# A two-stage kernel whose split operands move to rows 0 and 64 and whose instruction order comes from a planner of its own

## The chip, the cores and the metric

The kernel runs on one core of one Trainium2 chip. The metric is the device time of one execution in microseconds (us); the time before is the median of three runs. A core has five instruction queues that each run in order: TensorE (PE, with its weight loads shown as PEld), VectorE (DVE), ScalarE (ACT), GpSimd (POOL) and SyncE (SP, which here issues all DMAs).

## The reference

Inputs r, k, v, w, a, b have the shape 4 batches x 8 heads x 768 steps x 40. A 40x40 state per batch and head is carried through 768 steps, and its readings go through two dense blocks.

```python
for t in range(S):
    y[:, :, t] = np.einsum('bhd,bhde->bhe', rt, state)
    Sa = np.einsum('bhde,bhe->bhd', state, at)
    state_decay = state * wt[:, :, None, :] - np.einsum('bhd,bhe->bhde', Sa, bt)
    state = state_decay + np.einsum('bhd,bhe->bhde', vt, kt)
...
h = x @ w_in;  g = h * (1.0 / (1.0 + np.exp(-h)));  x = g @ w_out     # first block, 320 -> 2048 -> 320
h = x @ w_in;  g = h - np.tanh(h);                  return g @ w_out  # second block, own weights
```

The weights of the blocks arrive as 64-bit floats; the output is 3072 x 320 in fp32.

## The kernel before

The 768 steps are cut into 12 chunks of 64. Within a chunk the recurrence is solved with matrix products, so that only the 40x40 states pass from chunk to chunk. The 32 states (batch x head) are two halves `hf` of 16, and a half is two groups `u` of 8. Most fp32 factors are split into a high and a low fp16 number.

The stages of a chunk are small functions inside `build`, which are also the names used below. `load_raw` and `prep` bring in the inputs, form running products of w (two scans on DVE), scale the factors and split them into the tile HL; 24 DMAs per chunk then lay HL out as the tile LR. `p1` and `p2` multiply and transpose these factors on PE. `sol_in`, 31 times `sol_step` (two DVE instructions each, one waiting for the other) and `sol_out` solve a triangular system; `mrg1` and `mrg2` merge its 32-row blocks. Then comes the chain that carries the state: `ch_x` (PE) and `ch_xe` (ACT), `ch_u` (PE) and `ch_ue` (ACT and DVE, writes U), `ch_s` and `ch_se`, `ch_y` and `ch_ye` (writes the next transposed state MT), `ch_m` and `ch_me` (writes the next state M). `x_t1` and `x_t2` transpose the readings into the first block: `mm_h` (16 matmuls per hidden slice i of 8), `act1` (three ACT passes and one on POOL), `mm_o` (12 matmuls per i), `out1`, whose result goes to DRAM. When all chunks are done the second block runs: `mm_h`, `act2` and `mm_o` again, for 12 groups of tokens.

L (columns 0 to 193 of LR: decayed k and b, and u or v) and R (columns 194 to 321: a and r) hold three planes on 120 rows. L has high, high, low and R has high, low, high on rows 0 to 39, 40 to 79 and 80 to 119, so that one matmul with 120 rows sums high x high, high x low and low x high. MT and M have the same three planes. `ch_ue`, `ch_ye` and `ch_me` write the high plane to rows 0 to 39 and the low plane to a tile `lows`, and two DMAs each copy them to rows 40 to 79 and 80 to 119:

```python
ACT.activation(out=U[0:40, u], in_=pu, func=AF.Copy, scale=S_U)                                   # L398
DVE.scalar_tensor_tensor(out=Ul[:, u], in0=pu, scalar=S_U, in1=U[0:40, u], op0=ALU.mult, ...)     # L399
for p0, src in ((40, U[0:40]), (80, Ul)):
    SP.dma_start(out=U[p0:p0 + 40]..., in_=src...)                                                # L401
```

Two things set the order of instructions. The functions are called in the order of a time that the table `SC` gives each (8 units to a chunk, L687 onward); the framework's own scheduler, which has a model of the engines, then orders the instructions of each queue. The conversion of the first block's weights (`conv_w1`, 32 calls of `conv_f32` and what follows it) is tied behind instructions of chunk 0 (`gates`). LR tiles come from a ring of 5 buffers, which the second block's weights (`conv_w2`) use after chunk 11.

Of the kernel before, what the change touches and what calls it, by code (L numbers as in the profile page):

```python
# [9 lines left out]
I32 = mybir.dt.int32  # L10
# [14 lines left out]
RW = LW + 2 * C  # L25

# [80 lines left out]
def build(tc, pk, tv, w1i, w1o, w2i, w2o, out, nch=NCH, dbg=None):  # L107
# [16 lines left out]
    lrp = top.enter_context(tc.tile_pool(name="lrp", bufs=5))  # L124
# [14 lines left out]
    istk = const.tile([120, 40], F16, name="istk")  # L139
    POOL.memset(istk, 0.0)  # L140
    for base in (0, -80):
        POOL.affine_select(out=istk, in_=istk, compare_op=ALU.not_equal, fill=1.0, base=base,
                           pattern=[[-1, 40]], channel_multiplier=1)
# [20 lines left out]
    TT_t = [at_p.tile([128, 32, C], F32, name=f"TT{q}") for q in range(2)]  # L164
    mK_t = [at_p.tile([128, 4, 8, C], F32, name=f"mK{q}") for q in range(2)]
    for q in range(2):
        POOL.memset(mK_t[q][64 * q:64 * q + 64], 0.0)
        DVE.memset(TT_t[q], 0.0)
    VU_s = [at_p.tile([128, 2, DM], F32, name=f"VU{q}") for q in range(2)]
    Xs_s = [at_p.tile([128, 8, D], F32, name=f"Xs{q}") for q in range(4)]  # L170
# [4 lines left out]
    zo = const.tile([128, 2], F32, name="zo")  # L175
    POOL.memset(zo[:, 0:1], 0.0)
    POOL.memset(zo[:, 1:2], 1.0)
    tmp = at_p.tile([128, 136], F32, name="tmp")

    lows = at_p.tile([104, 32 * D], F16, name="lows")  # L180
    HL = at_p.tile([120, 6, 2 * RW], F16, name="HL")

    def planes(HL):
        return [HL[:, :, o:o + n] for o, n in ((0, LW), (LW, 2 * C), (RW, LW), (RW + LW, 2 * C))]

    DVE.memset(planes(HL)[0][:, :, 3 * C:LW], 0.0)
# [4 lines left out]
    gates = {}  # L191
# [9 lines left out]
    def load_raw(c, hf):  # L201

        spare = lr_slot().rearrange("p u n -> p (u n)").bitcast(F32)[0:120] if c == 0 and hf == 1 else None
# [12 lines left out]
    def prep(c, hf):  # L216
        w, ra, rkb, rrv = raw_t.pop((c, hf))
        hl = HL
        if c == 0 and hf == 1:
            hl = lr_slot().rearrange("p u n -> p (u n)")[0:120, 0:12 * RW].rearrange("p (j n) -> p j n", j=6)  # L220
            DVE.memset(planes(hl)[0][:, :, 3 * C:LW], 0.0)
# [48 lines left out]
    def p1(c, b):  # L270
# [47 lines left out]
    def sol_step(c, j):  # L318
# [5 lines left out]
        if c == 0:  # L324
            gates["dve"] = nc.cur_bb.bb.instructions[-1]

    def sol_out(c):
# [3 lines left out]
        TT = TT_t[c % 2]  # L331
# [28 lines left out]
    def mrg2e(c, hf):  # L360
        bb = 64 * (c % 2)
        ACT.activation(out=TT_t[c % 2][bb:bb + 32, hf * 16:hf * 16 + 16, 32:64], in_=ps_t["mg2", c][64 * hf:64 * hf + 32],
                       func=AF.Copy)

    def ch_x(c, hf):
        ps = ps_a.tile([128, 8, D], F32, tag="a", name="psx")
        for p in range(8):
            if c:
                for u in range(2):
                    PE.matmul(ps[64 * u:64 * u + 64, p, :], R_t[c, hf][:, u, p, 0:C], MT_t[c, hf][:, u, p, :], start=True, stop=False)  # L370
# [5 lines left out]
    def ch_xe(c, hf):  # L376
        bb = 64 * (c % 2)
        ps = ps_t.pop(("x", c, hf))
        for u in range(2):
            t = Xs_s[(4 * c + 2 * hf + u) % 4]  # L380
# [3 lines left out]
    def ch_u(c, hf):  # L384
        t = [ps_t.pop(("Xs", c, hf, u)) for u in range(2)]
        ps = ps_a.tile([128, 8, C], F32, tag="a", name="psu")
        for p in range(8):
            for u in range(2):
                PE.matmul(ps[64 * u:64 * u + 40, p, :], t[u][:, p, :], TT_t[c % 2][:, hf * 16 + u * 8 + p, :], start=True, stop=True)
        ps_t["u", c, hf] = ps  # L390

    def ch_ue(c, hf):
        ps = ps_t.pop(("u", c, hf))
        U_t[c, hf] = lows[0:40, 0:16 * C].rearrange("p (u j n) -> p u j n", u=2, n=C)
        U, Ul = L_t[c, hf][:, :, :, C:2 * C], U_t[c, hf]
        for u in range(2):
            pu = ps[64 * u:64 * u + 40]
# [397 lines left out]
```

## Time and profile before

| | |
|---|---|
| median of 3 runs | 1195.06 us (1190.68 to 1195.49) |
| the profiled execution | 1191.78 us, of which the span is 1190.0 us |
| mean granted TensorE clock | 0.924 of 2.4 GHz |
| PE / DVE / ACT / POOL busy | 78% / 72% / 74% / 43% of the span |
| PE weight loads busy | 63% of the span |

The span has four parts. Up to 173 us there is almost no dense work: chunk 0 is computed and the weights are converted. From there to 785 us the other chunks and the first block run side by side. Then follows the rest of the first block with the first matmuls of the second, to 874 us, and the second block alone to the end. The busy time of matmuls is modelled at its end, so that a PE that is always busy can still be waiting a little before each short matmul.

### The profile page before, as it was taken

The page shows a single profiled execution, that of the slowest core. Times are in us where ns is not written, and L with a number is a line of the kernel's source. Part 1 is how long each engine was busy: PE and PEld are TensorE (multiplying, and loading weights), DVE is VectorE, ACT ScalarE, POOL GpSimd, SP SyncE. Part 2 cuts the span into 40 slices and gives each one's busy share as a digit, 9 for nine tenths or more (in the row PEclk, how much of TensorE's full clock was granted, in tenths as well). Part 3 has the DMA queues.
Part 4 walks back from the last instruction along what each step waited for, and adds up shares of the span by engine and source line. Part 5 has one row for each costly group of instructions (what it writes and reads, how often), then busy time and mean ns, then how long its engine had stood idle before and what let it go on. Part 6 is the DMA issues. An engine that isn't in the chain of part 4 may idle for free.

```text
span 1190.0 us, 32101 instructions
## 1 busy us (share of the span) xinstructions
PE 930.4 (78%) x12624; PEld 754.0 (63%) x12624; DVE 860.6 (72%) x1752; ACT 886.4 (74%) x1718; POOL 508.7 (43%) x550
## 2 busy tenths in 40 slices
PE   0004327878888888897888888888999999999997
PEld 0004326657766666676766766776778888888885
DVE  6677878677877687787778757443188878888885
ACT  2468689757676677576757798998678888888885
POOL 5354564444444454454544334444333333333332
PEclk9999559888889898999889999999989999999999
DMA  6676765444435444445444333344011111111001
GB/s 161 183 199 176 187 171 140 111 118 117 125 99 138 107 119 115 123 113 124 115 108 123 79 105 96 108 124 120 14 27 37 25 26 25 26 31 32 13 12 23
DMA packets 181192, 115.85 MB, mean 97 GB/s; under 512 B 107121, under 2 KB 165553, under 8 KB 181041
## 3 DMA queue, kind: packets, MB, share of 16 engines
q1 hardware_dynamic: 181040, 113.80, 36.5%
q8 instruction: 99, 1.62, 0.6%
q14 instruction: 53, 0.43, 0.1%
HBM read 58.34 MB, written 12.58 MB: 60 GB/s over the span
## 4 chain that ended last, share of the span: by engine, by line
issue 20%; DMA 17%; PE 16%; ACT 15%; DVE 14%; SPq 10%; POOL 9%; POOLq 0%; DVEq 0%; ACTq 0%
POOL gl L196 7%; SPq L256 6%; PE hp L576 6%; DMA LR<-HL 4%; DMA pd<-pq 3%; ACT cr L532 2%; DVE tmp L321 2%; PE o L602 2%; DVE Tl L323 2%; PE o L600 2%; DMA LR<-lows 2%; PE o L601 2%; DVE pq L230 2%; DVE lows L399 2%; DMA x2d<-x2o 1%
## 5 line engine op out<-in xcount | busy, mean ns | idle before, releaser
L576 PE MATMUL hp<-xh,wih 128*128 128x256 f16 x960 | 196.4, 292 | 19.5 <-ACT hs L585 19.5
L196 POOL TENSOR_TENSOR gl<-q,gh 128x512 f16<-128x512 f32 x96 | 111.9, 1167 | 205.6 <-ACT gh L635 205.6
L576 PE MATMUL hp<-x,LR 128*128 128x256 f16 x1344 | 188.7, 274 | 1.9 <-DVE t L633 1.2
L196 POOL TENSOR_TENSOR gl<-hs,gh 128x512 f16<-128x512 f32 x96 | 113.9, 1186 | 150.0 <-ACT hs L587 100.0
L576 PEld LDWEIGHTS <-wih 128*128 128x128 f16 x1344 | 134.1, 104 | 46.2 <-issue 21.2
L576 PEld LDWEIGHTS <-LR 128*128 128x128 f16 x1344 | 132.1, 98 | 25.0 <-issue 2.4
L602 PE MATMUL o<-woh,gl 128*128 128x320 f16 x384 | 113.2, 308 | 8.6 <-POOL gl L196 8.5
L600 PE MATMUL o<-woh,gh 128*128 128x320 f16 x384 | 117.2, 307 | 3.3 <-ACT gh L586 2.1
L601 PE MATMUL o<-woh,gh 128*128 128x320 f16 x384 | 116.6, 306 | 0.0
L600 PE MATMUL o<-LR,gh 128*128 128x320 f16 x384 | 112.9, 302 | 1.3 <-ACT gh L635 1.3
L601 PE MATMUL o<-LR,gh 128*128 128x320 f16 x384 | 113.9, 302 | 0.0
L576 PE MATMUL hp<-xl,wih 128*128 128x256 f16 x384 | 112.2, 292 | 0.0
L321 DVE TENSOR_TENSOR tmp<-Al,Tl 128x126 f32<-128x126 f32 (+22 forms) x372 | 92.5, 249 | 19.2 <-ACT Al L312 10.0
L602 PE MATMUL o<-LR,gl 128*128 128x320 f16 x384 | 104.3, 302 | 0.5 <-POOL gl L196 0.5
L323 DVE TENSOR_TENSOR Tl<-Tl,tmp 128x126 f32<-128x126 f32 (+22 forms) x372 | 95.9, 258 | 9.1
L602 PEld LDWEIGHTS <-gl 128*128 128x128 f16 x768 | 75.4, 99 | 37.5 <-POOL gl L196 12.5
L630 DVE SCALAR_TENSOR_TENSOR s<-s,z 128x512 f32<-128x512 f32 x96 | 74.4, 775 | 33.2 <-ACT s L628 32.2
L600 PEld LDWEIGHTS <-gh 128*128 128x128 f16 x768 | 76.5, 100 | 31.9 <-ACT gh L586 2.7
L632 DVE SCALAR_TENSOR_TENSOR q<-hp,s 128x512 f32<-128x512 f32 x96 | 66.3, 691 | 38.2 <-POOL gl L196 26.2
L601 PEld LDWEIGHTS <-gh 128*128 128x128 f16 x768 | 76.3, 99 | 27.8 <-issue 1.4
L634 DVE COPY_PREDICATED q<-mk,t 128x512 f32<-128x512 int32 x96 | 79.2, 825 | 9.0
L276 PE MATMUL p1a<-LR 120*128 120x64 f16 x384 | 23.3, 211 | 78.6 <-DMA LR<-HL 54.6
(148 smaller groups left out, 2563.3 us busy)
## 6 DMA issues: line engine op xcount, KB each, us to landing
LR<-HL SPq DMA_DIRECT2D x92, 150.9 KB
rawkb<-pk SPq DMA_DIRECT2D x23, 360.0 KB
rawrv<-pk SPq DMA_DIRECT2D x23, 360.0 KB
cr<-w1i SPq DMA_DIRECT2D x16, 384.0 KB
cr<-w2i SPq DMA_DIRECT2D x16, 384.0 KB
cr<-w1o SPq DMA_DIRECT2D x16, 320.0 KB
cr<-w2o SPq DMA_DIRECT2D x16, 320.0 KB
LR<-HL SPq DMA_DIRECT2D x46, 100.6 KB
```

Source lines behind the costliest of these rows:

```text
L196: POOL.tensor_tensor(out, a, b, ALU.subtract)
L230: DVE.tensor_tensor_scan(pt[:, 0:390], w[:, 0:390], d1a.rearrange("p j t -> p (j t)"), 0.0, ALU.mult, ALU.add)
L256: SP.dma_start(out=dst[pl * 40:pl * 40 + 40, :, d0:d0 + w], in_=src[:, :, s0:s0 + w])
L321: DVE.tensor_tensor(tv_, Al[:, j + 1:, j:j + 1].to_broadcast([128, n, w]), Tl[:, j:j + 1, :w].to_broadcast([128, n, w]), ALU.mult)
L323: DVE.tensor_tensor(Tl[:, j + 1:, :w], Tl[:, j + 1:, :w], tv_, ALU.add)
L576: PE.matmul(o, wi[f][:, a], x[:, k], start=n == 0, stop=False)
L600: PE.matmul(o, gh[:, cs], wo[f][:, 0], start=f == 0, stop=False)
L601: PE.matmul(o, gh[:, cs], wo[f][:, 1], start=False, stop=False)
L602: PE.matmul(o, gl[:, cs], wo[f][:, 0], start=False, stop=f == NF - 1)
L630: DVE.scalar_tensor_tensor(out=s, in0=s, scalar=GAMMA, in1=z, op0=ALU.add, op1=ALU.mult)
L632: DVE.scalar_tensor_tensor(out=q, in0=hp, scalar=sh * S_G2, in1=s, op0=ALU.mult, op1=ALU.mult)
L634: DVE.copy_predicated(q, mk.bitcast(I32), t)
```

## The change

Four things change. The planes move: high on rows 0 to 39, low on rows 64 to 103, and rows 40 to 63 are zeroed once, so a product has 104 rows. R becomes two operands, R[0] with the high plane in both places and R[1] with the low plane in both, and each product with R takes two matmuls (`for q in range(2)`), which now sum all four combinations. ACT, DVE and POOL write U, MT and M straight into both places, and the 136 copies by DMA are gone; a layout of HL in 18 instead of 24 DMAs per chunk follows. In `ch_ue` and `ch_me` a call `apart` declares ACT's reading of group 1 independent of DVE's reading of group 0 in the same PSUM bank. LR is 4 fixed buffers (`LRS`) instead of a ring of 5, so chunk c's `prep` follows `ch_y` of chunk c - 2, and the second block's weights lie 5 to a buffer: numbers 0 to 4 in LRS[0], and so on, number 15 in LRS[3], which chunk 11's second half uses. MT and M have one buffer per half, Xs eight instead of four, TT one.

The order is planned. `kernel` builds the program three times: once to get its instructions and their dependencies, from which `plan` gives an order of the calls; once in that order, from which `plan` gives a sequence for each of the five queues, DMA issues included; and once more with each instruction of the first part of the program tied to its predecessor in its sequence. `plan` takes, again and again, the instruction with the longest way to the end among those that could start soonest, on the engine that is free first, with written costs per instruction. The second block (after `ph1.close()`) is not planned. `gates` is gone; `BOOST` puts `conv_w1` first.

```diff
+RX = RW + 2 * C
...
-    TT_t = [at_p.tile([128, 32, C], F32, name=f"TT{q}") for q in range(2)]
+    TT = at_p.tile([128, 32, C], F32, name="TT")
...
+    LRS = [lrp.tile([128, 16, RX], F16, name=f"LR{q}") for q in range(4)]
+    MTS = [at_p.tile([104, 2, 8, D], F16, name=f"MT{q}") for q in range(2)]
+    MS = [at_p.tile([104, 2, 8, D], F16, name=f"M{q}") for q in range(2)]
...
-            for pl, s0, d0, w in ((0, RW, 0, LW), (0, LW, LW, 2 * C), (1, RW, 0, RW), (2, 0, 0, RW)):
-                SP.dma_start(out=dst[pl * 40:pl * 40 + 40, :, d0:d0 + w], in_=src[:, :, s0:s0 + w])
...
+            for p0, s0, d0, w in ((0, 0, 0, RX), (64, LW, LW, 4 * C), (64, RX, 0, 3 * C)):
+                SP.dma_start(out=dst[p0:p0 + 40, :, d0:d0 + w], in_=src[:, :, s0:s0 + w])
+        LR = LR[0:104].rearrange("p (u j) n -> p u j n", u=2)
+        L, R = LR[:, :, :, 0:LW], (LR[:, :, :, LW:RW], LR[:, :, :, RW:RX])
...
-            PE.matmul(pa[:, p, :], kb, R[:, u, p, 0:C], start=True, stop=True)
+            for q in range(2):
+                PE.matmul(pa[:, p, :], kb, R[q][:, u, p, 0:C], start=q == 0, stop=q == 1)
...
+            for q in range(2 if c else 0):
                 for u in range(2):
-                    PE.matmul(ps[64 * u:64 * u + 64, p, :], R_t[c, hf][:, u, p, 0:C], MT_t[c, hf][:, u, p, :], start=True, stop=False)
+                    PE.matmul(ps[64 * u:64 * u + 64, p, :], R_t[c, hf][q][:, u, p, 0:C], MTS[hf][:, u, p, :], start=q == 0, stop=False)
...
         for u in range(2):
-            pu = ps[64 * u:64 * u + 40]
-            ACT.activation(out=U[0:40, u], in_=pu, func=AF.Copy, scale=S_U)
-            DVE.scalar_tensor_tensor(out=Ul[:, u], in0=pu, scalar=S_U, in1=U[0:40, u], op0=ALU.mult, op1=ALU.subtract)
-        for p0, src in ((40, U[0:40]), (80, Ul)):
-            SP.dma_start(out=U[p0:p0 + 40].rearrange("p u j n -> p (u j) n"), in_=src.rearrange("p u j n -> p (u j) n"))
+            pu, U = ps[64 * u:64 * u + 40], L_t[c, hf][:, u, :, C:2 * C]
+            i = ACT.activation(out=U[0:40], in_=pu, func=AF.Copy, scale=S_U)
+            if u:
+                apart(i, last)
+            last = DVE.scalar_tensor_tensor(out=U[64:104], in0=pu, scalar=S_U, in1=U[0:40], op0=ALU.mult, op1=ALU.subtract)
...
-            PE.matmul(ps[:, p, :], uv, R_t[c, hf][:, u, p, C:2 * C], start=True, stop=True)
+            for q in range(2):
+                PE.matmul(ps[:, p, :], uv, R_t[c, hf][q][:, u, p, C:2 * C], start=q == 0, stop=q == 1)
...
-                psub(ml[:, u], md, MT[0:40, u])
-            SP.dma_start(out=MT[40:80], in_=MT[0:40])
-            SP.dma_start(out=MT[80:120], in_=ml)
+                psub(MT[64:104, u], md, MT[0:40, u])
...
-        SP.dma_start(out=M[40:80], in_=M[0:40])
-        SP.dma_start(out=M[80:120], in_=ml)
...
+            last = DVE.tensor_tensor(M[64:104, u], pu, M[0:40, u], ALU.subtract)
...
-            t = lr_slot().rearrange("p u n -> p (u n)")[:, 0:4 * 1280].rearrange("p (f n) -> p f n", f=4)
-            w2.extend(t[:, q] for q in range(4))
+            t = LRS[f // 5].rearrange("p u n -> p (u n)")[:, 0:5 * 1280].rearrange("p (f n) -> p f n", f=5)
+            w2.extend(t[:, q] for q in range(5))
...
+BOOST = {"conv_w1": 100000}
+SPLIT = {"h1": 8, "o1": 6}
...
+    while any(ready.values()):
+        best = None
+        for e, r in ready.items():
...
+        t, n = max((q for q in c if q[0] <= t + LOOK[e]), key=lambda q: (us[q[1]].rank, -q[1]))
...
+        if e == "DVE" and u.two:
+            if busy[0] <= t < busy[1]:
+                f = max(f, busy[1] + min(u.cost, 90))
...
+    order, _ = traced(None)
+    _, seq = traced(order)
...
+        for _, v in seq:
+            for x, y in zip(v, v[1:]):
+                tc.add_manual_dep(ins[y], ins[x].name, info, reason="planned order")
```

Three places show what moves. On PE, where `ch_y` ends and `ch_s` of the next group begins, before (psm is the state's product, pss the product of U and v with R, psu their transpose by an identity `istk`):

```order
L431 MATMUL psy<-M,LR 64x40
L442 MATMUL psm<-VU_127,KBt 40x40 x15
L409 LDWEIGHTS LR
L409 MATMUL pss<-LR 128x64
L410 LDWEIGHTS LR
L410 MATMUL psu_4959<-istk,LR 128x40
```

and such a place now:

```order
L449 MATMUL psm<-VU_125,KBt 40x40 x16
L416 LDWEIGHTS LR_152
L416 MATMUL pss<-LR_152 128x64
L416 LDWEIGHTS LR_152
L416 MATMUL pss<-LR_152 128x64
L417 LDWEIGHTS LR_152
L417 MATMUL psu_6418<-istk,LR_152 128x40
```

The same weights are loaded twice, and the product with R is two matmuls.

On SP, in the middle of the program before, where U is copied (L401), the dense block's result leaves (L613), the next HL is laid out (L256) and MT is copied (L457, L458):

```order
L401 DMA LR<-lows 40x16x64
L613 DMA x2d<-x2o 128x2x384
L256 DMA LR<-HL 40x6x194
L256 DMA LR<-HL 40x6x128
L213 DMA VU_127<-tv 64x640
L256 DMA LR<-HL 40x6x322 x2
L256 DMA LR<-HL 40x6x194
L256 DMA LR<-HL 40x6x128
L256 DMA LR<-HL 40x6x322
L457 DMA MT<-MT 40x640
L256 DMA LR<-HL 40x6x322
L458 DMA MT<-lows 40x640
```

and such a place now (L268 lays out HL, L494 and L496 fetch factors for `x_t2`, L623 is the dense block's result):

```order
L268 DMA LR_151<-HL 40x6x192 x2
L268 DMA LR_151<-HL 40x4x192
L494 DMA pf<-pd 128x2x128
L496 DMA pf<-pd 64x128
L623 DMA x2d<-x2o 128x2x384
L268 DMA LR_151<-HL 40x6x450
L268 DMA LR_151<-HL 40x6x256
L268 DMA LR_151<-HL 40x6x450
L268 DMA LR_151<-HL 40x6x256
L268 DMA LR_151<-HL 40x4x450
L268 DMA LR_151<-HL 40x4x256
L226 DMA VU_125<-tv 64x640
```

No copy of U, MT or M stands in the queue any more; every DMA in it brings in inputs, lays out HL or carries a result away.

On DVE, at the start before, after the memsets (L230 to L245 are `prep` of chunk 0):

```order
L230 SCALAR_TENSOR_TENSOR pq<-raww,d1a 120x390
L231 RECIPROCAL d1b<-pq 120x6
L232 TENSOR_SCALAR HL<-pq 120x6
L235 SCALAR_TENSOR_TENSOR rawa<-rawa,pq 120x384
L236 SCALAR_TENSOR_TENSOR pr<-raww,d1b 120x389
L233 SCALAR_TENSOR_TENSOR HL<-pq,HL 120x6
L239 TENSOR_TENSOR rawkb<-rawkb,pr 120x768
```

and now (L535 and L537 belong to `conv_f32`, the conversion of weights):

```order
L242 SCALAR_TENSOR_TENSOR pq<-raww,d1a 120x390
L535 TENSOR_SCALAR cr<-cr 128x384
L243 RECIPROCAL d1b<-pq 120x6
L247 SCALAR_TENSOR_TENSOR rawa<-rawa,pq 120x384
L248 SCALAR_TENSOR_TENSOR pr<-raww,d1b 120x389
L537 SCALAR_TENSOR_TENSOR c_174<-c_174,cr 128x384
L251 TENSOR_TENSOR rawkb<-rawkb,pr 120x768
```

Weight conversion stands among the very first instructions, where before it began only with chunk 1's `prep`; by the end of chunk 0's part (`x_t2` of its second half) DVE has passed 19 whole pairs of it, against 27 before.

## Rows read from the trace of the kernel before

**Rows 1.** The page: busy times, 40 slices (PE, clock, GB/s), one costly group.
```profile
PE 930.4 (78%) x12624; PEld 754.0 (63%) x12624; DVE 860.6 (72%) x1752; ACT 886.4 (74%) x1718; POOL 508.7 (43%) x550
...
PE   0004327878888888897888888888999999999997
...
PEclk9999559888889898999889999999989999999999
...
GB/s 161 183 199 176 187 171 140 111 118 117 125 99 138 107 119 115 123 113 124 115 108 123 79 105 96 108 124 120 14 27 37 25 26 25 26 31 32 13 12 23
...
L276 PE MATMUL p1a<-LR 120*128 120x64 f16 x384 | 23.3, 211 | 78.6 <-DMA LR<-HL 54.6
```

**Rows 2.** Stages: length; busy us (instructions) per engine; granted clock, DMA share, GB/s.
```profile
0.00:173.00 173.00, 35.87 (x722) 32.21 (x724) 125.28 (x278) 102.56 (x197) 83.18 (x115) 0.84 0.67 177
173.00:261.00 88.00, 66.22 (x1139) 52.87 (x1133) 65.77 (x159) 68.23 (x135) 41.97 (x43) 0.87 0.52 136
261.00:478.00 217.00, 181.20 (x3081) 148.65 (x3079) 162.72 (x373) 151.34 (x304) 98.78 (x103) 0.89 0.44 115
478.00:654.00 176.00, 146.59 (x2530) 118.06 (x2528) 135.71 (x310) 120.29 (x245) 83.02 (x83) 0.92 0.46 118
654.00:785.00 131.00, 112.20 (x1922) 91.30 (x1920) 81.51 (x215) 113.65 (x234) 56.44 (x72) 0.96 0.36 100
785.00:874.00 89.00, 79.30 (x720) 63.20 (x719) 34.27 (x59) 69.52 (x134) 37.03 (x45) 0.94 0.26 72
874.00:1190.00 316.00, 309.00 (x2534) 247.71 (x2532) 255.35 (x363) 260.78 (x474) 108.26 (x93) 0.99 0.12 26
```

**Rows 3.** Timeline of DVE: the first U written in chunk 2 and chunk 9.
```profile
251.33 0.68 DVE L399 SCALAR_TENSOR_TENSOR lows<-psu,LR 40x512 f16<-40x512 f32 x1
...
666.21 0.68 DVE L399 SCALAR_TENSOR_TENSOR lows<-psu,LR 40x512 f16<-40x512 f32 x1
```

**Rows 4.** Waits: who waited for whom, us in total, times, longest.
```profile
PE p1a L276 <- DMA LR<-HL: 54.6, 8, 22.7
...
PE mg L342 <- DVE W L333: 49.1, 5, 28.3
...
ACT LR L398 <- DVE lows L399: 33.2, 14, 4.4
...
PE pss L409 <- DMA LR<-lows: 27.8, 11, 13.6
```

**Rows 5.** The critical chain in order of time: start, us, what.
```profile
495.75 2.80 DMA LR<-lows
```

**Rows 6.** Tile lows: SP's own time per DMA, ns min/median/max, first and last start.
```profile
L401 SPq DMA_DIRECT2D LR<-lows x24: 767/798/1056, 122.7 to 785.8; - x24
L458 SPq DMA_DIRECT2D MT<-lows x22: 731/757/868, 143.1 to 757.9; - x22
```

**Rows 7.** Timeline of PE: start, us until a run's last matmul ends, shape, count.
```profile
479.92 0.20 PE L370 MATMUL psx<-MT,LR 120*64 120x40 f16 x2
...
479.95 0.29 PE L372 MATMUL psx<-VU,mK 128*64 128x40 f32 x4
...
528.75 0.40 PE L276 MATMUL p1a<-LR 120*128 120x64 f16 x8
...
645.92 0.64 PE L276 MATMUL p1a<-LR 120*128 120x64 f16 x8
```

**Rows 8.** Groups of DVE instructions: count, busy us, mean ns, idle before them.
```profile
L533 DVE SCALAR_TENSOR_TENSOR c<-c,cr 128x384 int32<-128x384 int32 (+1 forms) x64 | 37.2, 582 | 25.0 <-ACT cr L532 23.4 <-POOL wih L196 0.8 <-POOL x2o L612 0.5
...
L230 DVE TENSOR_TENSOR_SCAN pq<-raww,d1a 120x390 f32<-120x390 f32 x23 | 32.8, 1425 | 5.7 <-DMA pd<-pq 4.0 <-DMA raww<-pk 1.3
...
L531 DVE TENSOR_SCALAR cr<-cr 128x384 int32<-128x384 int32 (+1 forms) x64 | 26.5, 418 | 26.8 <-ACT c L530 26.4
...
L168 DVE MEMSET TT<- 128x2048 f32 x2 | 3.5, 1765 | 1.7 <-PEq L786 1.3 <-issue 0.4
```

**Rows 9.** Line L230 by itself: ns min/median/max, first and last start.
```profile
L230 DVE TENSOR_TENSOR_SCAN pq<-raww,d1a x23: 970/1212/2362, 9.2 to 640.2; 120x390 f32<-120x390 f32 x23
```

More of the change, by code (lines that the diff above doesn't have):

```diff
@@ L167, in build @@
         POOL.memset(mK_t[q][64 * q:64 * q + 64], 0.0)
-        DVE.memset(TT_t[q], 0.0)
     VU_s = [at_p.tile([128, 2, DM], F32, name=f"VU{q}") for q in range(2)]
-    Xs_s = [at_p.tile([128, 8, D], F32, name=f"Xs{q}") for q in range(4)]
+    Xs_s = [at_p.tile([128, 8, D], F32, name=f"Xs{q}") for q in range(8)]
     for t in VU_s + Xs_s:
@@ new lines, in latency_of, with units_of @@
+def latency_of(i, e, cost):
+    if e == "PE":
+        return cost + 170
+    if e == "SP":
+        o = i.outs[0]
+        name = o.bass_ap.tensor.name
+        return 4300 if name[:3] in ("raw", "cr_", "VU_") or name.startswith("LR") and o.ap[0][1] != 40 else 3000
+    return cost
+class Unit:
+    __slots__ = ("e", "ins", "cost", "late", "succ", "pred", "rank", "ready", "name", "args", "tiles", "tiled", "two", "left", "hold", "holds", "start")
+def units_of(tc, ins, marks):
+    at = {i.name: k for k, i in enumerate(ins)}
+    n1 = marks[-1][0]
+    task = [(-1, "init", ())] * n1
+    for (a, nm, ar), (b, _, _) in zip(marks, marks[1:]):
+        task[a:b] = [(a, nm, ar)] * (b - a)
+    us, of, cur = [], [], {}
+    for k in range(n1):
+        i = ins[k]
+        e = ENGINES.get(str(i.engine))
+        if not i.outs or not hasattr(i.outs[0], "ap"):
+            e = None
+        t = task[k]
+        u = cur.get(t[0]) if e == "PE" else None
+        if u is None or len(us[u].ins) >= SPLIT.get(t[1], 999):
+            u = len(us)
+            v = Unit()
+            v.e, v.ins, v.cost, v.late, v.succ, v.name, v.args = e, [], 0, 0, set(), t[1], t[2]
+            v.tiles, v.tiled, v.two = set(), False, False
+            us.append(v)
+            if e == "PE":
+                cur = {t[0]: u}
+        of.append(u)
+        v = us[u]
+        v.ins.append(k)
+        if e:
+            c = cost_of(i, e)
+            v.cost += c
+            v.late = latency_of(i, e, v.cost)
+            v.two = e == "DVE" and sum(hasattr(q, "ap") and "PSUM" not in str(q.bass_ap.space) for q in i.ins) > 1
+            v.tiled = e == "PE" and tuple(i.tile_size or (128, 128)) != (128, 128)
+        v.tiles |= {t.name for t in tile_rust.get_accessed_tiles(i, tc.info.uid)}
+    for k in range(n1):
+        for d in ins[k].descendants or ():
+            d = at[d]
+            if d < n1 and of[d] != of[k]:
+                us[of[k]].succ.add(of[d])
+    return us
@@ new lines, in order_of @@
+def order_of(us):
+    key = [(u.name,) + u.args for u in us]
+    when, left, after = {}, {}, {}
+    for n, u in enumerate(us):
+        k = key[n]
+        if u.e:
+            when[k] = min(when.get(k, (u.start, n)), (u.start, n))
+        left.setdefault(k, 0)
+        after.setdefault(k, set()).update(key[m] for m in u.succ if key[m] != k)
+    for v in after.values():
+        for k in v:
+            left[k] += 1
+    todo = [(when.get(k, (0, 0)), k) for k, c in left.items() if not c]
+    heapq.heapify(todo)
+    order = {}
+    while todo:
+        _, k = heapq.heappop(todo)
+        order[k] = len(order)
+        for m in sorted(after[k], key=str):
+            left[m] -= 1
+            if not left[m]:
+                heapq.heappush(todo, (when.get(m, (0, 0)), m))
+    assert len(order) == len(left)
+    return order
```

330 lines of the change are left out of this document (267 added, 63 removed).

## The prediction

> **What bounds the kernel now.** I read the page's busy times and slices first [rows 1], then a table by stage [rows 2], and only then the waits. The reader is to see that no engine is full before 830 us: PE is busy 930.4 of 1190.0 us, and from 874 us on it is busy 309.00 of 316.00 us, so that last stage is its own limit and the change does not touch it. The 259.6 us in which PE is idle are the account I work in. By stage they are 173.00 - 35.87 = 137.1 us before the first dense matmul, then 21.8, 35.8, 29.4 and 18.8 us up to 785 us (105.8 together), then 9.7 and 7.0 us [rows 2]. They add up to the 259.6.
>
> In the middle stages two engines are near each other: from 478 to 654 us PE is busy 146.59 of 176.00 us (83%) and DVE 135.71 (77%), ACT 120.29, POOL 83.02 [rows 2]. The pace there is seen in the first U of chunk 2 and of chunk 9: (666.21 - 251.33) / 7 = 59.3 us per chunk [rows 3]; scaled to it, PE works 49.4 and DVE 45.7 us per chunk. Neither sets the pace alone; what fails is that work which is ready stands behind work that waits, in queues that run in order. The waits name some of it: PE waits 27.8 us in 11 pieces for the copies of U, 54.6 us in 8 for the layout of LR (its longest piece, 22.7 us, belongs to the start) and 49.1 us in 5 for the solve's transpose [rows 4].
>
> The clock adds to that. The granted share is 0.87, 0.89, 0.92 and 0.96 in the four middle stages [rows 2]; with levels of 1.2 and 2.4 GHz, twice the missing share is time at the lower one: 22.9 + 47.7 + 28.2 + 10.5 = 109 us.
>
> **The copies.** 136 DMAs go (48 of U, 44 of MT, 44 of M). On SP each holds the queue for about 0.8 us [rows 6], and a landing takes 2.80 us on the chain [rows 5]. Their direct worth is what PE waits for them, 27.8 us [rows 4]; I take -28, with 0 as the small end, if another wait ends at the same moment (DVE's writing of the low plane stays), and no more than 28. The wait of ACT for DVE between the two groups of U, 33.2 us in 14 pieces [rows 4], goes with `apart`. I give it nothing: ACT has a third of its time free, and what PE loses by it is already inside the 27.8; if that cover were gone it would be part of the term below. The lighter SP queue (about 105 us less issuing, and six fewer DMAs per chunk for LR) is priced with the order.
>
> **The added matmuls.** `p1` and `ch_s` take 384 more each, `ch_x` and `ch_y` 352 more each: 1472. Eight matmuls of `p1` end 0.40 us after the first starts, one lasts 0.211, so they follow at (0.40 - 0.21) / 7 = 27 ns; at the lower clock at (0.64 - 0.21) / 7 = 61 ns [rows 1, 7]. A pair in `ch_x` holds the next back by 0.03 us [rows 7]. At the high clock: 768 x 0.027 + 352 x 0.03 = 31 us; all at the lower one 768 x 0.061 + 352 x 0.06 = 68 us; if all fall into time in which PE is idle now, 0. I take 33, near the high-clock end, since that is the clock for most of the time. The other engines lose and gain no work per chunk that matters: the low planes are written by the same instructions to another place.
>
> **The order, start.** Before 173 us DVE is the engine with most work, 125.28 us [rows 2]. In the new order 8 pairs of weight conversion that stood ahead of chunk 0's end stand behind it (19 against 27); at 0.582 + 0.418 us that leaves 117 us [rows 8]. Bytes bound it as well: 177 GB/s over 173 us are 30.6 MB; less 8 loads of some 0.36 MB that is 27.7 MB, and at the best slice's 199 GB/s [rows 1] 139 us. I take 139, so -34 us. The ends: 117 us with no idle time at all (-56), or +5, if the conversions put first hold up chunk 0's own inputs. The new memsets ahead of DVE's first scan are 3600, 2048 and twice 640 columns; at 1765 ns for 2048 [rows 8] they end after 6.0 us, and the scan waits for its input until 9.2 us [rows 9], so they cost nothing while that input is late.
>
> **The order, middle.** Of the 105.8 us of idle PE, 28 are counted above. The other 78 are the prize of a better order. No other engine forbids filling them (the next, DVE, is at 77%), but PE and DVE both at four fifths collide often, and the written sequence fixes five queues with assumed landing times. I take half, -39, with ends of 0 and -78. The denser PE should also fall to the lower clock less often: of the 109 us half, 55 us, done in half the time, would be -27; since short matmuls with waits gain less, I take -17 (ends 0 and -30). LR in four fixed buffers delays a layout until the chunk two before is done; I see its price only as a wait for LR like the one in [rows 4], and it is inside the half that I leave.
>
> **The tail.** Weights 10 to 14 of the second block now wait for chunk 11's first half and number 15 for its second; before, 12 to 15 waited for the first. Idle time after 785 us is 16.7 us [rows 2]; I add 5 (ends -10 and +25, a conversion chain that PE would have to sit out).
>
> **Sum.** 1190.0 - 28 + 33 - 34 - 39 - 17 + 5 = 1110 us of span; the profiled execution has 1.8 us outside its span, so 1112 us. That execution (1191.78) is 3.3 us under the median, inside the spread of the three runs, and I add nothing for it.
>
> A page speaks against this account. The Trainium skill, "Trainium Kernel Development and Optimization", Performance Expectations, says that matmul busy time is a bad measure of how close PE is to its limit and that weight-load busy time is a good one. Weight loads are busy 754.0 us, and 118.06 of 176.00 us (67%) in the middle [rows 1, 2], against 83%. By that measure PE has room for the added matmuls at no cost, and the rival below that fills PE would come out near 1027 us; the trace leaves both open. The skill's "SBUF — State Buffer", Who interferes with whom, says that a DVE instruction with two SBUF inputs and a GpSimd one block each other in full; a denser schedule would then stretch more of the scans. They already spread from 970 to 2362 ns [rows 9], 10 us in all over their best; half as much again would be 5 us of DVE, which the sum leaves out, as DVE is not its limit.
>
> **The rivals.** First, PE never waits: the plan fills all 105.8 us, the clock gives 25, the start gives 34, the added matmuls cost 33 and the tail nothing. That is 1190 - 106 - 25 - 34 + 33 + 2 = 1060 us. For it: the states' chain is short without copies, and dense work is always at hand. Against it: DVE would need 45.7 us of a pace near 50.
>
> Second, the plan holds only on paper. Queues frozen with constant landing times stop as a whole when one transfer is late; the gain of 28 is eaten by the 33, and start and middle keep their idle time but for a few us: about 1190 us, no change. For it: landings vary within one kind of transfer. Against it: the present order is just as frozen on each queue.
>
> Third, slower: PE's added matmuls stand in the states' chain, where PE comes last and often at the lower clock, so they cost up to 68 us, and the new order saves nothing but the copies: 1190 - 28 + 68 + 2 = 1232 us. It decides as soon as order and clock give back less than the 5 to 40 us by which the matmuls exceed the copies. Against it: those are small beside 259.6 us of idle time. That the change doesn't do what it says I rule out: the order of PE and SP shows the doubled matmuls and no copies.
>
> **How the numbers follow.** The forecast has 0.60, with a range of its own from 1080 to 1150; PE never waiting 0.20 (1027 to 1080), the paper plan 0.11, slower 0.09. From 1052 to 1190 us lie the forecast, somewhat more than half of the first rival and half of the second, about 8 in 10. Half a per cent, 6 us, is about what a measurement of this kernel can tell from no change. Faster than that: 0.60 + 0.20 + 0.05 = 0.85; within it 0.06; slower 0.09.
>
> **What would show it.** Right: the first dense matmul near 139 us; U at a pace of about 54 us per chunk (612 us less 28, 39 and 17, plus 33, over the same chunks: 51 us in some 10 chunks); PE's idle time near 40 us between there and chunk 11, its clock above 0.95 there; 768 matmuls of `p1` at 27 ns; no wait of `pss` for a DMA. Wrong: idle time of PE as before behind new names (LR's layout, DVE's scans), the dense block starting at 173 us again, or a hole of over 25 us for the last weights after chunk 11.

## The result, and the profile after

The changed kernel takes 1140.58 us (median of 4 runs, 1140.02 to 1144.23) against 1195.21 us (median of 4 as well, one run more than in the table before), a ratio of 0.9558 with a 95% interval of 0.9528 to 0.9588. The prediction said 1112 us, with 1080 to 1150 for its own case: the direction and the case came true, but of the 83 us that it forecast only 54.6 came. The profiled execution took 1144.23 us, the slowest of the four, with a span of 1142.5 us. Of half_solve, among the experiments, one run of four was a slow one (1135.55 us), and its median of 1117.7 us leaves that run out.

The page after, busy times and slices (PE, clock), which answer to [rows 1]:

```profile
PE 956.4 (84%) x14096; PEld 782.2 (68%) x14096; DVE 861.0 (75%) x1756; ACT 896.0 (78%) x1721; POOL 513.4 (45%) x552
...
PE   0314668868898899998898998989999999999997
...
PEclk9999569896989989998989999999999999999999
```

PE has 26.0 us more busy time and 1142.5 - 956.4 = 186.1 us of idle time, where it had 259.6. DVE, ACT and POOL have nearly the work they had. The table by stage, with the columns of [rows 2]; its cuts are the first dense matmul (147.6 us), chunk 2's and about chunk 9's first U (214, 592), the last U (761) and the last result of the first block (828):

```profile
0.00:147.60 147.60, 44.57 (x902) 40.85 (x903) 117.11 (x267) 98.19 (x178) 72.88 (x103) 0.89 0.67 176
147.60:214.00 66.40, 56.45 (x1090) 46.14 (x1089) 53.77 (x123) 58.02 (x113) 33.85 (x36) 0.76 0.52 138
214.00:435.00 221.00, 188.93 (x3718) 154.76 (x3715) 184.56 (x434) 165.24 (x335) 106.60 (x109) 0.90 0.46 119
435.00:592.00 157.00, 140.39 (x2695) 114.18 (x2692) 118.55 (x287) 111.84 (x227) 77.24 (x76) 0.93 0.40 106
592.00:641.00 49.00, 43.77 (x893) 36.51 (x892) 39.14 (x97) 37.98 (x77) 24.97 (x26) 1.00 0.33 83
641.00:761.00 120.00, 109.70 (x1640) 89.73 (x1639) 61.59 (x139) 105.36 (x207) 57.30 (x71) 1.00 0.29 86
761.00:828.00 67.00, 65.40 (x646) 53.29 (x644) 31.60 (x53) 59.36 (x118) 32.26 (x38) 1.00 0.28 75
828.00:1142.50 314.50, 307.21 (x2530) 246.78 (x2527) 254.66 (x363) 260.00 (x474) 108.32 (x93) 1.00 0.11 25
```

PE's idle time is 147.60 - 44.57 = 103.0 us before the first dense matmul, then 10.0, 32.1, 16.6, 5.2 and 10.3 us up to the last U (74.2 together), 1.6 us in the rest of the first block and 7.3 us in the second.

The stretch from the first dense matmul to the last U is as long as it was, 613.4 us against 612: its idle time fell, but PE does 33 us more work in it (539.2 us busy against 506.2). The 47.5 us of span are gained at its two ends, 25.4 us before it and 23.5 us behind it.

The pace, as the first U of chunks 2 and 9 (timeline of DVE):

```profile
213.78 0.68 DVE L407 SCALAR_TENSOR_TENSOR LR<-psu,LR 40x512 f16<-40x512 f32 x1 [0.76 <-ACT LR L404]
...
591.35 0.68 DVE L407 SCALAR_TENSOR_TENSOR LR<-psu,LR 40x512 f16<-40x512 f32 x1 [3.18 <-ACT LR L404]
```

(591.35 - 213.78) / 7 = 53.9 us per chunk, where [rows 3] gave 59.3. But the dense block falls behind meanwhile: chunk 10's U comes at 640 us and chunk 11's only at 749, and the stretch between is dense work with PE at 91% and ACT at 88%.

PE's waits, who for whom, us in total, times, longest:

```profile
PE hp L580 <- ACT hs L589: 33.8, 27, 6.3
...
PE p1b L307 <- DMA LR<-HL: 28.5, 3, 24.6
...
PE mg L347 <- DVE W L338: 22.1, 6, 15.4
...
PE p1a L287 <- DMA pd<-pq: 20.9, 1, 20.9
...
PE p1a L287 <- DMA LR<-HL: 14.5, 14, 2.2
```

The waits of [rows 4] for the copies of U are gone, and the three longest single pieces lie in the start. Another name leads: the dense matmul `hp` waits for ACT's first pass (L589), which frees the one PSUM buffer of `hp`. That wait is not new, it has grown; before the change it was:

```profile
PE hp L576 <- ACT hs L585: 19.5, 18, 4.8
```

Its longest piece now is worth reading on two engines. PE's timeline (start, us, what, idle time before it):

```profile
256.16 0.27 PE L581 MATMUL hp<-xl,wih 128*128 128x256 f16 x1
262.75 0.37 PE L580 MATMUL hp<-xh,wih 128*128 128x256 f16 x1 [6.31 <-ACT hs L589]
262.92 0.42 PE L580 MATMUL hp<-xl,wih 128*128 128x256 f16 x1
```

and ACT's in the same stretch:

```profile
256.38 0.52 ACT L253 ACTIVATE HL<-rawa 120x384 f16<-120x384 f32 x1
256.81 0.51 ACT L255 ACTIVATE HL<-rawrv 120x384 f16<-120x384 f32 x1
258.36 0.59 ACT L299 ACTIVATE bP<-p1a 32x512 f32<-32x512 f32 x1 [1.04 <-DVE mK L295]
258.96 0.37 ACT L300 ACTIVATE bP<-p1a 32x256 f32<-32x256 f32 x1
259.34 0.52 ACT L256 ACTIVATE HL<-rawrv 120x384 f16<-120x384 f32 x1
259.89 1.25 ACT L336 ACTIVATE Al<-Tl 64x512 f32<-64x512 f32 x2
261.04 0.41 ACT L486 ACTIVATE M<-psm 40x320 f16<-40x320 f32 x1
261.48 0.60 ACT L321 ACTIVATE Tl<-zo 128x512 f32<-128x512 f32 x1
262.10 0.60 ACT L589 ACTIVATE hs<-hp 128x512 f32<-128x512 f32 x1
```

`hp` is complete at 256.4 us, but nine passes of other tasks stand ahead of L589 in ACT's queue, and one of them waits 1.04 us for DVE. PE is idle for 6.3 us, and behind the hole the granted clock is 0.50 (from 262.75 to 266.00 us), its 1.2 GHz level: a matmul takes 0.42 us where it took 0.27.

Of the smaller steps: 16 matmuls of `p1` end 0.64 us after the first starts, one lasting 0.19 us, so they follow at (0.64 - 0.19) / 15 = 30 ns (27 forecast, [rows 7]):

```profile
344.09 0.64 PE L287 MATMUL p1a<-LR 104*128 104x64 f16 x16
```

SP's DMAs of the layout keep their 0.8 us each (median 804 ns, as for the copies of [rows 6]); the copies' landing of [rows 5] has no counterpart. DVE's conversions are as in [rows 8] (583 ns; the other pass 516 ns, where it had 418) and the scan of [rows 9] has a median of 979 ns (1212 before) and a longest of 2297.

### The profile page after: what moved, and what is told of

It reads as the page before. It is cut to its first block, busy times and chain, and to the rows that moved or that the text cites. A ratio compares the mean times of both kernels' runs of the same rounds, so it can differ in the third digit from the quotient of the medians.

```text
span 1142.5 us, 34671 instructions
## 1 busy us (share of the span) xinstructions
PE 956.4 (84%) x14096; PEld 782.2 (68%) x14096; DVE 861.0 (75%) x1756; ACT 896.0 (78%) x1721; POOL 513.4 (45%) x552
## 4 chain that ended last, share of the span: by engine, by line
PE 28%; issue 19%; DVE 19%; ACT 15%; POOL 9%; DMA 8%; SPq 2%; POOLq 0%; DVEq 0%; ACTq 0%
PE hp L580 9%; POOL gl L209 7%; DMA LR<-HL 4%; DVE Tl L331 4%; DVE tmp L329 3%; PE o L604 3%; PE o L606 3%; PE o L605 3%; PE psu L393 2%; ACT hs L589 1%; SPq L268 1%; PE mg L360 1%; ACT cr L536 1%; ACT gh L590 1%; PE hp L581 1%
## 5 line engine op out<-in xcount | busy, mean ns | idle before, releaser
L580 PE MATMUL hp<-xh,wih 128*128 128x256 f16 x960 | 190.5, 286 | 40.2 <-ACT hs L589 33.8
L580 PEld LDWEIGHTS <-wih 128*128 128x128 f16 x1344 | 132.8, 102 | 72.7 <-issue 47.4
L209 POOL TENSOR_TENSOR gl<-hs,gh 128x512 f16<-128x512 f32 x96 | 117.4, 1224 | 126.8 <-ACT hs L591 90.9
L606 PE MATMUL o<-woh,gl 128*128 128x320 f16 x384 | 117.9, 307 | 0.8 <-POOL gl L209 0.8
L604 PE MATMUL o<-LR,gh 128*128 128x320 f16 x384 | 111.6, 299 | 1.4 <-ACT gh L645 1.3
L605 PE MATMUL o<-LR,gh 128*128 128x320 f16 x384 | 112.7, 299 | 0.0
L580 PE MATMUL hp<-xl,wih 128*128 128x256 f16 x384 | 109.8, 286 | 1.4 <-POOL xl L209 1.4
L640 DVE SCALAR_TENSOR_TENSOR s<-s,z 128x512 f32<-128x512 f32 x96 | 73.5, 766 | 31.1 <-ACT s L638 30.3
L636 ACT ACTIVATE z<-hp 128x512 f32<-128x512 f32 x96 | 57.8, 603 | 32.0 <-PE hp L581 32.0
```

The lines of the kernel that those rows point to most:

```text
L209: POOL.tensor_tensor(out, a, b, ALU.subtract)
L580: PE.matmul(o, wi[f][:, a], x[:, k], start=n == 0, stop=False)
L604: PE.matmul(o, gh[:, cs], wo[f][:, 0], start=f == 0, stop=False)
L605: PE.matmul(o, gh[:, cs], wo[f][:, 1], start=False, stop=False)
L606: PE.matmul(o, gl[:, cs], wo[f][:, 0], start=False, stop=f == NF - 1)
L636: ACT.activation(out=z, in_=hp, func=AF.Square, scale=sh)
```

## The experiments

Times are medians; ratios are to the kernel before on the same chip. "Idle" is span less PE's busy time, "middle" its part from the first dense matmul to the last U, in the profiled execution. Every run from three_a on and the changed kernel itself are built with a plan of their own, so a planned variant differs from the changed kernel in its whole order and not only in the lines shown; costs_fit, which changes nothing but written costs, is 47 us away. raw_single, three_a and kb_on_pool lie between 1137 and 1147 us. What a planned variant takes is measured; that a difference of some 20 us comes from its edit, and not from its plan, no run shows.

| kernel | us | ratio, 95% | PE busy | idle | middle | first dense | pace |
|---|---|---|---|---|---|---|---|
| before | 1195.2 | 1 | 930.4 | 259.6 | 105.8 | 173.2 | 59.3 |
| changed | 1140.6 | 0.956 (0.953-0.959) | 956.4 | 186.1 | 74.2 | 147.6 | 53.9 |
| layout_only | 1225.8 | 1.028 (1.023-1.034) | 964.4 | 257.7 | 92.4 | 188.7 | 61.8 |
| calls_only | 1212.1 | 1.018 (1.012-1.023) | 983.9 | 226.9 | 93.4 | 161.8 | 61.1 |
| three_a | 1142.9 | 0.959 (0.954-0.963) | 953.5 | 187.8 | 71.4 | 161.3 | 56.2 |
| tl_sbuf | 1203.9 | 1.008 (1.006-1.011) | 952.1 | 252.0 | 87.7 | 196.2 | 60.7 |
| two_banks | 1220.5 | 1.022 (1.017-1.028) | 959.9 | 257.7 | 99.4 | 183.4 | 62.3 |
| raw_single | 1137.4 | 0.952 (0.947-0.957) | 949.7 | 191.9 | 72.4 | 171.1 | 53.1 |
| half_solve | 1117.7 | 0.937 (0.931-0.943) | 947.1 | 172.5 | 65.6 | 154.4 | 52.3 |
| no_low_R | 1120.2 | 0.940 (0.935-0.945) | 907.7 | 206.0 | 67.7 | 176.2 | 50.8 |
| kb_on_pool | 1147.3 | 0.963 (0.958-0.968) | 956.2 | 191.9 | 78.0 | 167.0 | 52.9 |
| copies_back | 1156.1 | 0.967 (0.963-0.972) | 960.1 | 188.6 | 76.9 | 156.2 | 54.3 |
| no_boost | 1169.9 | 0.979 (0.975-0.983) | 965.8 | 201.0 | 100.5 | 135.0 | 58.1 |
| costs_fit | 1187.5 | 0.994 (0.992-0.996) | 967.4 | 215.8 | 103.0 | 143.8 | 58.2 |

**Layout without the plan (layout_only).** The three builds become one, with `build(tc, *args)` and no order; `gates` is back.

> The new layout (rows 0 and 64, no copies, two products with R, four fixed LR buffers) with the old way of ordering: the table of times, the framework's scheduler, the conversions tied behind chunk 0. By the terms of the prediction it is the copies' -28 and the matmuls' +33 and a tail of up to +25: 1190 to 1220 us, so that the whole gain is the order's. Rival (the layout is worth most of it): 1150 to 1170 us, first dense matmul still near 173 us.

1225.8 us, 31 us over before and 6 us above the first range. On this layout the whole gain is the order's, and the layout by itself costs; the order on the old layout was not run. PE's busy time is 34 us more, at nearly the clock of before (0.928 against 0.924): the price of the added matmuls, forecast at 33. The idle time is 1.9 us less: 13.4 less in the middle, lost again in the start and after the last U.

**The order of the calls alone (calls_only).** The loop that ties each instruction to its predecessor is left out:

```
-        for _, v in seq:
-            for x, y in zip(v, v[1:]):
-                tc.add_manual_dep(ins[y], ins[x].name, info, reason="planned order")
```

> The calls in the planned order, but no instruction tied to its predecessor, so that the framework's scheduler orders each queue. If the order of the calls is what the plan gives, 1140 to 1150 us; if the five sequences matter (SP's issues and the mixing of conversions with chunk 0 on DVE and ACT), 1160 to 1200 us, with a first dense matmul after 155 us.

1212.1 us, a little beyond the second range. The planned order of calls gives 14 us of the 85 between layout_only and the changed kernel, the five tied sequences 71.5. In the profiled executions that is 40.8 us of PE's idle time and 27.5 us of its busy time, at a granted clock of 0.925 against 0.943.

**A second buffer for hp (two_banks, tl_sbuf, three_a, raw_single).**

```
-    Tl = ps_s.tile([128, 32, 16], F32, name="Tl")
+    Tl = at_p.tile([128, 32, 16], F32, name="Tl")          # two_banks, tl_sbuf
-    ps_h = ...tc.tile_pool(name="ps_h", bufs=1, space=PSUM)
+    ps_h = ...tc.tile_pool(name="ps_h", bufs=2, space=PSUM) # two_banks, three_a
-    ps_a = ...tc.tile_pool(name="ps_a", bufs=4, space=PSUM)
+    ps_a = ...tc.tile_pool(name="ps_a", bufs=3, space=PSUM) # three_a
-        ("w", 1920, 391, 2), ("a", 0, 384, 2)
+        ("w", 1920, 391, 1), ("a", 0, 384, 1)               # two_banks, tl_sbuf, raw_single
```

> The changed kernel with two PSUM banks for the dense block's first product hp instead of one; the bank comes from the solve's tile Tl, which moves to SBUF, and raww and rawa have one buffer instead of two to make room. Theory (the missing part of the gain is one bank): in the changed kernel PE waits 33.8 us in 27 pieces for ACT's first pass over hp (L589) between 147.6 and 761 us. With a second bank that wait goes, and the time is 1140 - 30 = 1110 us, between 1100 and 1120. Rival (shared work is the limit: DVE is busy 84% of 214 to 435 us, PE 86%): the wait only changes its name, PE's idle time between the first dense matmul and chunk 11's U stays near 74 us, and the time is 1130 to 1145 us.

> The control: Tl in SBUF and one buffer for raww and rawa, but still one bank for hp. Both theories expect 1135 to 1150 us; the solve's instructions (L329, 248 ns, and L331, 257 ns) stay within 10% unless the place of Tl matters, in which case they become longer and the time rises by up to 15 us.

> The second bank for hp taken from the pool of the attention's products (three banks instead of four), everything else as in the changed kernel. One-bank theory: the wait for L589 goes as well, worth 30 us, against what the chains lose with three banks; 1110 to 1140 us. Shared work: the chains lose and nothing is won, 1145 to 1180 us.

> The changed kernel with one buffer instead of two for raww and rawa, as in the control with Tl in SBUF (1203.86 us) and in the kernel with copies below; order planned anew. If Tl's place is what cost the 63 us there (the solve's DVE time rose by 95 us in all), 1135 to 1150 us. Rival: the two input buffers cost it, above all in the start (first dense matmul at 196 us there): 1175 to 1205 us with the dense block after 175 us.

The first theory fell: the wait can be cut and the time stays. three_a cuts the wait for L589 from 33.8 to 12.9 us:

```profile
PE hp L580 <- ACT hs L589: 12.9, 9, 5.7
```

and its time is the same (1142.9), its middle idle time 71.4 us instead of 74.2. The gaps ahead of `mm_h` fall there from 36 to 14 us, and those ahead of `ch_s` rise from 6 to 15 and ahead of `mm_o` from 1 to 6. two_banks is to be compared with its control tl_sbuf, which has one buffer:

```profile
PE hp L579 <- ACT xh L514: 28.6, 6, 11.5
...
PE hp L579 <- ACT hs L588: 17.4, 28, 1.8
```

In two_banks the wait falls from 17.4 to 5.4 us, and the wait for the chunk's result that the dense block reads (L514) grows from 28.6 to 43.1:

```profile
PE hp L579 <- ACT xh L514: 43.1, 8, 10.1
...
PE hp L579 <- ACT hs L588: 5.4, 3, 2.1
```

two_banks is slower than its control by 17 us. The control itself was a surprise, 66 us over raw_single (1137.4), which is as fast as the changed kernel, so that the input buffers are cleared. What is left is the place of Tl, and with it another plan, since `plan` reckons with which DVE instructions have two inputs in SBUF (`u.two`). DVE's solve in raw_single:

```profile
L331 DVE TENSOR_TENSOR Tl<-Tl,tmp 128x126 f32<-128x126 f32 (+22 forms) x372 | 95.5, 257 | 7.8
L329 DVE TENSOR_TENSOR tmp<-Al,Tl 128x126 f32<-128x126 f32 (+22 forms) x372 | 92.2, 248 | 14.0 <-ACT Al L320 5.7
```

and in tl_sbuf:

```profile
L330 DVE TENSOR_TENSOR Tl<-Tl,tmp 128x126 f32<-128x126 f32 (+22 forms) x372 | 152.3, 409 | 6.7
L328 DVE TENSOR_TENSOR tmp<-Al,Tl 128x126 f32<-128x126 f32 (+22 forms) x372 | 143.6, 386 | 33.4 <-ACT Al L319 26.9
```

The same 744 instructions take 108 us more, 9 us per chunk (the 95 us of raw_single's expectation are the rise of DVE's whole busy time, 861.0 to 956.7), and the pace grows from 53.1 to 60.7 us. So most of what was added to DVE came out in the pace, although DVE is busy only 80% from 214 to 592 us in the changed kernel. 25 of the 66 us lie ahead of the first dense matmul (196.2 us against 171.1), where the first two chunks' solves take 16 us more (47.4 against 31.1). How much of the 66 us is the longer instructions and how much the other plan, no run separates.

**Less for DVE (half_solve, kb_on_pool).** `if j % 2: return` in `sol_step`; and `(DVE if c == 0 else POOL).tensor_tensor(kbv, ...)` in `prep`.

> Leaves out the odd steps of the triangular solve (15 of 31 pairs of DVE instructions per chunk), nothing else; order planned anew. By L329 (248 ns) and L331 (257 ns) DVE has 15 x 0.505 = 7.6 us less per chunk. Theory (DVE sets the pace, as the pace of 61.9 us in the control with Tl in SBUF suggests, where DVE's solve grew by about 8 us per chunk): the pace falls from 53.9 us by 5 to 7.6 us until PE's own 47 us per chunk hold it, and the time is 1140 - 10 x 5 to 10 x 7 = 1070 to 1090 us. Rival (PE with its waits for one bank and the queues' fixed order set it): pace 52 to 54 us, time 1125 to 1140 us.

> From chunk 1 on the product rawkb x pr of prep (L251, 1166 ns on DVE, twice a chunk) is done by POOL; nothing is left out. If DVE sets the pace, 2.3 us less per chunk: pace about 51.6 us, time 1115 to 1125 us. If not, 1135 to 1145 us. If POOL, which then has about 3.4 us more per chunk, delays the low planes it writes or blocks DVE's instructions with two SBUF inputs, 1145 to 1160 us.

half_solve takes 69.5 us from DVE (861.0 to 791.5) and gains 23 us, not 50 to 70, between the two ranges: the pace falls by 1.6 us only, and the middle idle time by 8.6. (The control's pace, 61.9 us in the expectation, is 60.7 by the table's measure.) kb_on_pool is 7 us slower (1147.3 us), inside the last of its three ranges: DVE's busy time falls by 10.9 us and POOL's rises by 25.5, and the pace falls by 1.0 us without a gain. DVE alone is not the bound either: 108 us more in its solve came with 66 us more, 69.5 us less with 23 us less.

**Less for PE (no_low_R).** `for q in range(2)` becomes `R[0]` alone in `p1`, `ch_x`, `ch_s` and `ch_y`.

> Leaves out every product with R[1] (the low plane of R), 1472 matmuls; order planned anew. By the prediction's term (33 us on PE's path) the time is about 1107 us. If DVE sets the pace, PE's lighter load is worth only what it does at the start and after chunk 11: 1125 to 1140 us, pace 52 to 54 us. PE's busy time should fall by about 30 us in both.

1120.2 us, between the two, and 20.4 us under the changed kernel by the medians. PE's busy time falls by 48.7 us, more than the 30 expected. In the profiled executions (the slowest of the changed kernel, the fastest here) 28.8 us of these reach the end, and the idle time grows by 19.9 us: 21 us in the start (124.2 us before the first dense matmul, at 176.2 us) and 5 after the last U, with 6.5 us less in the middle.

**The copies (copies_back).**

```
-            last = DVE.scalar_tensor_tensor(out=U[64:104], ...)
+            last = DVE.scalar_tensor_tensor(out=Ul[:, u], ...)
+        SP.dma_start(out=L_t[c, hf][64:104, :, :, C:2 * C]..., in_=Ul...)     # MT and M alike
```

> The low planes of U, MT and M are again written to a tile of 40 rows and carried to rows 64 to 103 by one DMA each (68 DMAs, planned like all others); raww and rawa have one buffer, so it is to be compared with raw_single. By the prediction's term the copies are worth 28 us: 20 to 30 us above raw_single, with waits of pss for a DMA near 20 us. Rival: the plan puts other work beside the landings, 0 to 10 us above it.

(The input buffers are those of raw_single.) 18.7 us above raw_single, between both: the 68 copies, planned like all else, come with that much, and the runs of the two do not overlap (1150.6 to 1159.4 us against 1131.0 to 1143.3). Their waits in the trace (the profiled execution is 5.5 us under the median) come to 10.6 and 5.3 us:

```profile
PE pss L418 <- DMA LR<-lows: 10.6, 3, 6.0
...
PE psx L374 <- DMA MT<-lows: 5.3, 2, 3.2
```

**What the plan is told (no_boost, costs_fit).** `BOOST = {}`; and in `cost_of`, PE's figures times 1.15, 1140 for 960 and `100 + 1.1 * n` for `60 + .76 * n` on DVE.

> BOOST empty: the conversions of the first block's weights are no longer put first. Theory (the start's gain of 25 us comes from putting them first): chunk 0's first U comes before 100 us, but the first dense matmul waits for weights or the dense block is interrupted, PE's idle time before 214 us is 15 to 30 us more than the 113 of the changed kernel, 1150 to 1170 us. Rival (any plan mixes them in as well): 1135 to 1145 us.

> The changed kernel with the planner's written costs nearer to the trace: PE's times 1.15 (hp's matmuls 122 ns measured between 214 and 592 us, 109 written), DVE's scans 1140 instead of 960 ns, its one-input passes 522 instead of 352 ns at 384 columns. Theory (the plan leaves PE 74 us of idle time after the start because its costs are too low): idle time falls to 50 us or less, 1110 to 1125 us. Rival (any such plan leaves 65 to 80 us, as in the four planned variants so far): 1130 to 1150 us.

no_boost starts the dense block 12.6 us earlier than the changed kernel (135.0 us) and is 29 us slower. The time is in the theory's range, but not for its reason: PE's idle time before 214 us is 111.8 us, 1 us less than in the changed kernel and not 15 to 30 more. The loss is in the middle, where the idle time is 26 us more and PE waits for the converted weights:

```profile
PE hp L580 <- ACT hs L589: 18.7, 19, 3.5
PE hp L580 <- ACT wih L543: 11.3, 4, 5.4
PE o L604 <- ACT woh L551: 8.2, 4, 2.9
```

costs_fit contradicts both theories: with costs nearer to the trace the plan loses 47 us of the gain of 54.6. Its middle idle time is 103.0 us, near that of before, with `hp` waiting longer for ACT:

```profile
PE hp L580 <- ACT hs L589: 44.8, 34, 5.0
```

## Why the prediction was right, and where it was too high

The prediction rested on an order that fills PE's idle time, with a layout that by itself takes as much as it gives. The runs show the first part: layout alone +31 us, order -85. The second holds less well: the matmuls cost what was forecast, but the copies' 28 us did not show by themselves: PE's idle time in layout_only is only 1.9 us under that of before. Rival three had priced "the new order saves nothing but the copies" at 1232 us; without the order the layout takes 1225.8. Rival two (a plan on paper) is what costs_fit comes close to in time, at 1187.5, though not in kind: it keeps the gain of the start (99.7 us idle there) and loses the middle's.

Term by term, from the stage table, in the profiled executions:

| term of the sum | forecast | measured |
|---|---|---|
| start: idle before the first dense matmul | -34 | 137.1 to 103.0: -34.1 |
| copies and middle idle: 105.8 us less 28 and 39 | -67 | 105.8 to 74.2: -31.6 |
| PE's busy time: matmuls +33, clock -17 | +16 | 930.4 to 956.4: +26.0 |
| tail: idle after the last U | +5 | 16.7 to 8.9: -7.8 |
| sum | -80 | -47.5 |

**The step that failed is the middle**, "I take half, -39", added to the copies' -28: 31.6 us of idle time went instead of 67. Two of the prediction's signs failed with it: PE's idle time between the first dense matmul and the last U was to be near 40 us and is 74.2, and the clock there was to be above 0.95 and is 0.92. The prediction saw that PE and DVE at four fifths collide often, and still let half of the waits go. The plan did remove the waits it was aimed at: with PE's gaps in the middle summed by the function of the matmul that ends them, before the change 21 us stood ahead of `p2` and 18 ahead of `ch_s`, after it 6 and 6. But those ahead of `mm_h` rose from 19 to 36 us. Taking the wait for `hp` away did not give it back (three_a, two_banks), and taking 69.5 us of work from DVE gave back 8.6 (half_solve): every plan with the written costs and the boost kept 66 to 78 us in the middle, tl_sbuf and two_banks more. That the idle time moves between names is shown. Why about 70 us remain is argued only: three queues at 73 to 87% that run in order and wait for one another's results.

**The clock** hardly came back where it was forecast. From the first dense matmul to the last U twice the missing share is 31.9 + 44.2 + 22.0 = 98 us at the lower level, against 109; holes like that at 256 us, behind which the clock is low, are still there. Over the whole span it is 130 us against 181 (2 x 0.057 x 1142.5 and 2 x 0.076 x 1190.0), so most of what came back lies in the start and after the last U. In PE's busy time the term can be estimated at 8 us of the 17, if layout_only (964.4) is taken as the changed kernel (956.4) with the clock of before. The term was doubtful in another way too: three_a has a granted clock of 0.967 over its span against 0.943, which is 2 x 0.024 x 1142 = 55 us less time at the lower level, and its PE busy time is only 2.9 us less, its time the same.

**The matmuls** were sized well (34 us of busy time in layout_only), and the p1 spacing came near the forecast (30 ns against 27, in one run of 16). **Two figures came true in part by luck.** The pace is 53.9 us where 54 was forecast, but that was worked out from a stretch that would shrink by 51 us, and the stretch did not shrink (613.4 us against 612): the chunks up to 10 pass sooner, and chunk 11's first U then comes 109 us after chunk 10's, where it came 51 us after it before. The start's idle time came out to the figure, -34, though the first dense matmul came at 147.6 us and not at 139: 25.4 us are the earlier beginning, and 8.7 us are more work of PE before it (44.57 us busy against 35.87). Nor is the reason given the whole of it: I had dense work begin earlier because fewer conversions stand ahead of chunk 0, whereas no_boost, with conversions not put first, begins at 135.0 us and loses, and raw_single begins at 171.1 us and does not. The moment of the first dense matmul says little. That what counts is whether the weights are there when the dense block runs is argued from no_boost's 19.5 us of waits for them, and not shown by a run of its own. The tail, forecast at +5, came out at -7.8 and hid 13 us of the middle's miss.

The copies were sized at 28. Bringing 68 of them back, half as many as before, cost 19 us under a plan. The scans, which a denser schedule was to stretch, did not (979 ns against 1212 in the median). No wait for the last weights came after chunk 11: 1.6 us of idle time there.

On the measure of PE, the rows of no_low_R bear on a rule that spoke against the sum. Taking away 1472 matmuls took 44.5 us of weight loads and 48.7 us of matmul busy time, and the time fell by 20.4 us, though weight loads were busy for 68% of the span. The added matmuls were not free, as far as two plans can be compared, and busy matmul time overstates them (28.8 us of span between the two profiled executions, 20.4 between the medians). The Trainium skill, "Trainium Kernel Development and Optimization", Performance Expectations, calls matmul busy time a bad measure and weight-load busy time a good one; the rows of no_low_R agree with the first half. By the second, as the prediction read it, a PE with its loads busy for 68% had room for these matmuls at no cost, and taking them away should not have shortened the time; here the measured 20 us decide.

What stays open: why the costs nearer to the trace give so much worse a plan. No run separates PE's factor from DVE's. The written costs act here as a setting that fits, not as estimates.

## What to carry to other kernels

When no engine is full and PE waits in many short pieces, price an order by what share of that idle time other versions of the same kernel kept, not by what no engine forbids: in layout_only, three_a and two_banks a named wait was taken away or cut, and PE's idle time stayed or grew. The layout that frees transfers by doubling matmuls cost 31 us by itself here; it was timed as a gain only together with the order. And a plan with written costs has to be timed anew after each change of its costs, since here three changed costs took away almost the whole gain.

## What the runs showed of the hardware

The place of one small operand changed the time more than a second PSUM buffer did. With Tl in PSUM, the solve's second instruction takes 159 ns at the least, 266 in the median, 308 at the most (raw_single); with Tl in SBUF beside another SBUF operand it is nearly the same in the median, with a long tail:

```profile
L330 DVE TENSOR_TENSOR Tl<-Tl,tmp x372: 173/273/1697, 52.6 to 779.6; 128x126 f32<-128x126 f32 x18, 128x30 f32<-128x30 f32 x12, 128x56 f32<-128x56 f32 x12, 128x78 f32<-128x78 f32 x12
```

The tail stands beside POOL. Of these 372 instructions 217 run while POOL does nothing, and they take 246 ns on average and 301 at the most; the other 155 overlap with an instruction of POOL and take 638 ns on average, and all 84 that take over 500 ns are among them. In raw_single the same two averages are 249 and 262 ns. The longest one begins just after a pass of POOL over 768 columns and ends just after it:

```profile
290.08 1.59 POOL L256 TENSOR_TENSOR HL<-rawkb,HL 120x768 f16<-120x768 f32 x1 [0.75 <-ACT HL L251]
290.11 1.70 DVE L330 TENSOR_TENSOR Tl<-Tl,tmp 128x108 f32<-128x108 f32 x1
```

In two_banks, with Tl in SBUF as well, one of the solve's first instructions (L328) takes 6.34 us, beside several passes of POOL that follow one another from 612.1 to 618.4 us. The Trainium skill, "SBUF — State Buffer", Who interferes with whom, says that a DVE instruction with two SBUF inputs contends with a GpSimd instruction that reads SBUF; the trace agrees, and prices it at 108 us over 744 instructions. The whole time was 66 us longer, with another plan.
